# Softmax maximum taken as a minimum, and another order of two steps of the second layer

## The chip, the cores and the metric

The kernel runs on one core of a Trainium2 chip. The metric is the device time of one execution in microseconds (us); the median of three runs before the change is 1177.47 us. Engines are named as in the profile: PE (TensorE matmul), PEld (its weight loads), DVE (VectorE), ACT (ScalarE), POOL (GpSimd), SP (SyncE, which issues DMAs).

## The reference

Attention with a causal window of 128 and 4 sink positions (4 batches, 8 heads, 768 positions, head size 64), then two feed-forward layers on 3072 tokens of width 512: one dense, one with 8 experts of which each token takes one.

```python
scores = scale * q @ k.T                      # scale = 1/8
scores = where(is_sink | in_window, scores, -1e9)
a = exp(scores - max(scores)); a = a / (sum(a) + 1e-9)
x = (a @ v) as 3072 x 512
h = maximum(x @ w_in, 0); x = h * h @ w_out   # 512 -> 2048 -> 512
e = argmax(x @ w_gate)                        # 8 experts
y = maximum(x @ w1[e], 0) @ w2[e]             # 512 -> 1024 -> 512
out = softmax weight of e * sigmoid(x @ w_output_gate)[e] * y
```

## The kernel before

Matrices are float32. Products are made of three reduced-precision matmuls: each operand is split into a high part (a copy, mostly by ACT) and a remainder (a subtraction, mostly by DVE), and high x high, high x remainder and remainder x high are summed in PSUM.

**First layer.** The tokens go in 12 blocks `t` of 256; each block has attention for 4 head pairs `p` and two halves `n`, so 8 score steps, 96 in all. `scores` makes the products into PSUM (two heads `e`, up to 260 columns), adds the mask and takes the row maximum in one DVE instruction for each head (L425; the row value is written by a second, small DVE instruction under the same line), multiplies the two maxima by -SCALE (L427, DVE), takes the exponential with that as bias and sums the row (L429, ACT), adds 1e-9 (L431), inverts (L432), and scales the probabilities (L439 or L441). The sink columns go to `psk` (L444 to L446, POOL). `ptrans` transposes on PE (L458), `pv` multiplies by v (L499 or L492). `fin_sink` transposes `psk` (L516, PE) when the last of a block's 8 steps has filled it. The dense layer is `l1` (L566) and `l2` (L582), 16 steps a block, between which the attention of the next block is strewn by due times (`attn_events`, `run_to`). During block 0 the weights of the dense layer are converted, 32 pieces, each with three steps on ACT (L283, L284, L289; every third piece has the last one on DVE, L291), two on DVE (L286, L287) and one on POOL (L292). In this whole part the order on each engine is chosen by a planner from priorities and its own estimate of the times; `high_priority` blocks are moved ahead.

**Second layer.** The tokens are sorted by expert: `place` computes each token's place (PE L669 and L670, DVE L671 to L676) and POOL scatters the token numbers to the table `perm` (L678). `slots` computes which expert each of up to 31 slots of 128 tokens has. `places(s)` loads a slot's token numbers (SP, L855), `gather(s)` fetches the rows by an indirect DMA (POOL, L859), `xtr(s)` transposes them (PE L874, ACT L868, DVE L877), `m_l1` and `htr` make the hidden layer (PE L888, ACT L894; PE L901, ACT L868, DVE L904), `m_l2` the output (PE L917) whose second half scales it (ACT L925) and scatters the rows to the result (POOL L926). `split_raw` converts a quarter of the next expert's weights (DVE L841 and L842) and `load_raw` loads the following one (SP). This part stands under `manual_schedule`: each engine takes its instructions in the order of the code. Slots 0 and 1 are taken before all tokens are placed (they hold only tokens already placed); slot 2 (`PRE`) is the first that needs the last block's placing. The order around the change is L1048 to L1084.

A function given as `mid` to `m_l1` is called between the groups of three matmuls of one quarter of the inner dimension: before the change ahead of the third group.

Of the kernel before, what the change touches and what calls it, by code (L numbers as in the profile page):

```python
# [13 lines left out]
AF = mybir.ActivationFunctionType  # L14
ALU = mybir.AluOpType
# [12 lines left out]
SCALE = 1.0 / float(D) ** 0.5  # L28
# [14 lines left out]
def kern(ctx, tc, q, k, v, n_sink, window, w_in, w_out, w_gate, w_og, w1, w2, out):  # L43
    nc = tc.nc
    V, A, G, PE, SY = nc.vector, nc.scalar, nc.gpsimd, nc.tensor, nc.sync
# [36 lines left out]
    def fill(o, n):  # L82

        w = o.shape[-1]
        for _ in range(n):
            PE.matmul(o, lhsT=idle[:, 0:128], rhs=idle[:, 0:w], start=True, stop=True)
# [315 lines left out]
    def scores(t, p, n):  # L402
        i = 2 * (t % 3) + n
        W = 128 if i == 0 else 260
        c0 = KS * n if i else KS
        mask = (M0, M1, M2)[min(i, 2)]
        qt = qTt[t, p]
        kt = kTt[t, p]
        if t == 0 and n % 2:
            ps = [psX.tile([128, 512], F32, tag=f"x{e}", name=f"psx{e}") for e in range(2)]  # L410
        else:
            ps = [psS.tile([128, 260], F32, tag=f"s{e}", name=f"pss{e}") for e in range(2)]
        if t == 0:
            fill(ps[0][:, 0:W], 2)
        for e in range(2 if t < T32 else 0):
            r = slice(64 * e, 64 * e + 64)
            PE.matmul(ps[e][:, 0:W], lhsT=qt[r, 0, n, :].bitcast(F32), rhs=kt[r, 0, c0:c0 + W].bitcast(F32), start=True, stop=True)
        for m, (a_, b_) in enumerate(((0, 0), (0, 1), (1, 0)) if t >= T32 else ()):
            for e in range(2):
                r = slice(64 * e, 64 * e + 64)  # L420
                PE.matmul(ps[e][:, 0:W], lhsT=qt[r, a_, n, :], rhs=kt[r, b_, c0:c0 + W], start=(m == 0), stop=(m == 2))  # L421
        P = att.tile([128, 2, 260], F32, tag="P", name="P", bufs=2)
        st = att.tile([128, 8], F32, tag="st", name="st", bufs=4)
        for e in range(2):
            V.tensor_tensor_reduce(out=P[:, e, 0:W], in0=ps[e][:, 0:W], in1=mask[:, 0:W], scale=1.0, scalar=-3.0e38,  # L425
                                   op0=ALU.add, op1=ALU.max, accum_out=st[:, e:e + 1])
        V.tensor_scalar(out=st[:, 2:4], in0=st[:, 0:2], scalar1=-SCALE, scalar2=None, op0=ALU.mult)  # L427
        for e in range(2):
            A.activation(out=P[:, e, 0:W], in_=P[:, e, 0:W], func=AF.Exp, scale=SCALE, bias=st[:, 2 + e:3 + e],  # L429
                         accum_out=st[:, 4 + e:5 + e])  # L430
        V.tensor_scalar(out=st[:, 6:8], in0=st[:, 4:6], scalar1=1e-9, scalar2=None, op0=ALU.add)  # L431
        V.reciprocal(out=st[:, 6:8], in_=st[:, 6:8])  # L432
        if t >= T32 and i >= 2:

            V.tensor_tensor(out=P[:, :, 0:128], in0=P[:, :, 0:128], in1=P[:, :, 132:260], op=ALU.add)
            W = KS
        for e in range(2):
            if t < T32 and t + e:
                V.tensor_scalar(out=P[:, e, 0:W], in0=P[:, e, 0:W], scalar1=st[:, 6 + e:7 + e], scalar2=None, op0=ALU.mult)  # L439
            else:  # L440
                A.activation(out=P[:, e, 0:W], in_=P[:, e, 0:W], func=AF.Copy, scale=st[:, 6 + e:7 + e])  # L441
        if i >= 2:
            o = psk[n][:, 2 * p:2 * p + 2, :]
            G.tensor_copy(out=o[:, :, 0:4], in_=P[:, :, 128:132])  # L444
            G.tensor_copy(out=o[:, :, 8:12], in_=P[:, :, 128:132])
            G.tensor_tensor(out=o[:, :, 4:8], in0=P[:, :, 128:132], in1=o[:, :, 0:4].bitcast(F32), op=ALU.subtract)  # L446
        Ptile[t, p, n] = P
# [416 lines left out]
    def copy_out(o, i, branch):  # L864
        if branch:
            V.tensor_copy(out=o, in_=i)
        else:
            A.activation(out=o, in_=i, func=AF.Copy)  # L868

    def xtr(s, br=False):  # L870
        x = xg[s]
        ps = pC.tile([128, 4, 128], F32, tag="ht", name="psxt") if s < PRE else pA.tile([128, 4, 128], F32, tag="x", name="psxt")
        for kk in range(4):
            PE.transpose(ps[:, kk], x[:, 128 * kk:128 * kk + 128], ident[:])  # L874
        o = xtt[s % 2]
        copy_out(o[:, 0], ps[:], br)
        V.tensor_tensor(out=o[:, 1], in0=ps[:], in1=o[:, 0].bitcast(F32), op=ALU.subtract)  # L877
        xt2[s] = o

    def m_l1(s, n, par, br=False, mid=None):  # L880
        o = xt2[s]
        ps = pB.tile([128, 512], F32, tag="h", name="psh2")
        c = 0
        for kk in range(4):
            if kk == 2 and mid:
                mid()
            for a_, b_ in ((0, 0), (0, 1), (1, 0)):
                PE.matmul(ps[:], lhsT=o[:, a_, kk, :], rhs=wview(n, par + 2048 * b_ + 512 * kk, 512), start=(c == 0), stop=(c == 11))  # L888
                c += 1
        r = m3.tile([128, 512], F32, tag="r", name="r2", bufs=2)  # L890
        if br:
            V.tensor_scalar(out=r[:], in0=ps[:], scalar1=0.0, scalar2=None, op0=ALU.max)
        else:
            A.activation(out=r[:], in_=ps[:], func=AF.Relu)  # L894
        hh_[s, n] = r
# [149 lines left out]
    with tc.manual_schedule():  # L1045
        pt = lambda: pD.tile([128, 4, 128], F32, tag="y", name="psg2")
        tr, tr1, lg, place = gate_pieces(NBLK - 1, pt)
        xtr(0)  # L1048
        xtr(1)
        tr()  # L1050
        tr1()
        m_l1(0, 0, 0)
        m_l1(0, 1, 0, mid=lg)
        htr(0, 0)
        m_l1(1, 0, 0, mid=place)
        rest = slots(pt())
        extra = cv.tile([128, 2, XW], F32, tag="stage", name="xg2", bufs=3)
        xgr.extend(extra[:, n] for n in range(2))
        places(PRE)
        gather(PRE)  # L1060
        htr(0, 1)
        m_l1(1, 1, 0)
        rest()
        for s in range(PRE + 1, PRE + 6):
            places(s)
        m_l2(0, 0, 0)
        gather(3)
        htr(1, 0)
        split_raw(1, 4096)
        load_raw(1, es[2], True)  # L1070
        m_l2(0, 1, 0)
        htr(1, 1)
        gather(4)
        m_l2(1, 0, 0)
        xtr(2)
        split_raw(3, 4096)
        load_raw(3, es[2], True)
        m_l2(1, 1, 0)
        for n in range(2):
            m_l1(2, n, par_of(2))  # L1080
            resplit(2, n)
        xtr(3)
        htr(2, 0)
        htr(2, 1)  # L1084
        for s in range(2, NT // 128 - 1):
            body(s)
        s = NT // 128 - 1
        for n in range(2):
            m_l2(s, n, par_of(s))
            resplit(s, 2 + n)  # L1090
        tail(s + 1)
# [28 lines left out]
```

## Time and profile before

| | |
|---|---|
| median of three runs | 1177.47 us (1174.87 to 1177.99) |
| the profiled execution | 1176.28 us, span 1174.4 us |
| PE busy | 1127.7 us, 96% |
| DVE busy | 755.4 us, 64% |
| ACT busy | 633.6 us, 54% |
| POOL busy | 451.8 us, 38% |
| granted TensorE clock, mean | 0.987 |

PE is the engine with the largest share. The shares are means over stages: up to about 152 us block 0's attention, the conversion of the weights and block 0's products; then eleven blocks alike up to about 780 us; then the last block and the joint to the second layer, up to about 845 us; then one slot after another. A line of a stretch gives its length and for each engine the busy time and the number of instructions; PEclk is the granted clock as a share of full speed. In a timeline each row has its start, its duration, engine, line and operation, and in brackets the engine's idle time before it and what ended that.

### The profile page before, as it was taken

What the parts mean: (1) busy time and instruction counts of PE and PEld (TensorE: products, weight loads), DVE (VectorE), ACT (ScalarE), POOL (GpSimd) and SP (SyncE); (2) the same over time, 40 slices, a digit from 0 to 9 for tenths busy, and PEclk for the clock granted to TensorE, in tenths of its full rate; (3) what the DMA queues carried; (4) which work ended last, traced back from release to release, by engine and by line L of the source; (5) the groups of instructions that cost most, each with busy time, mean ns of one, the idle gap of its engine ahead of it and who ended that gap; (6) DMA issues with size and microseconds to landing.
All of it is one profiled execution on the core that took longest, in us unless ns stands there. A gap on an engine that the chain in (4) does not pass through costs nothing. (4 is left out here: it accounts for less than half of the span.)

```text
span 1174.4 us, 24093 instructions
## 1 busy us (share of the span) xinstructions
PE 1127.7 (96%) x7079; PEld 946.6 (81%) x7082; DVE 755.4 (64%) x2114; ACT 633.6 (54%) x1750; POOL 451.8 (38%) x949
## 2 busy tenths in 40 slices
PE   7888899999999999999999999999899999999996
PEld 3566688888888888888888888887688888888884
DVE  5899777667676767676667676557411566863153
ACT  4777676767676767676776667454222222222200
POOL 4466564336464326565335655210211221221111
PEclk9899999999999999999999999999999999999998
DMA  5666311111111111211111110295411366654110
GB/s 129 188 180 184 100 28 46 37 51 36 49 30 46 35 48 37 55 32 28 51 37 49 38 42 1 28 246 158 126 38 46 120 199 225 211 197 141 40 50 23
DMA packets 139388, 100.10 MB, mean 85 GB/s; under 512 B 103903, under 2 KB 112223, under 8 KB 139234
## 3 DMA queue, kind: packets, MB, share of 16 engines
q1 hardware_dynamic: 132674, 83.85, 25.9%
q0 software_dynamic: 5472, 14.19, 3.7%
q8 instruction: 65, 1.06, 0.4%
q14 instruction: 89, 0.73, 0.3%
q10 hardware_dynamic: 1088, 0.26, 0.1%
HBM read 85.56 MB, written 13.76 MB: 85 GB/s over the span
## 5 line engine op out<-in xcount | busy, mean ns | idle before, releaser
L566 PE MATMUL psh<-xT,WI 128*128 128x256 f32 x2304 | 314.3, 285 | 10.6 <-POOL WI L292 7.0
L566 PEld LDWEIGHTS psh<-xT,WI 128*128 128x128 f32 x2304 | 296.5, 191 | 26.4 <-POOL WI L292 9.1
L888 PE MATMUL psh<-WI,xt 128*128 (+1 forms) x672 | 164.8, 399 | 0.3 <-ACT ht L868 0.3
L582 PE MATMUL psx<-WOa,h 128*128 128x512 f32 x576 | 160.3, 411 | 0.0
L582 PE MATMUL psx<-WOb,h 128*128 128x512 f32 x576 | 157.1, 408 | 1.2 <-ACT h L572 0.9
L888 PEld LDWEIGHTS psh<-WI,xt 128*128 128x128 f32 x672 | 124.1, 188 | 28.1 <-ACT xt L868 0.5
L570 DVE TENSOR_TENSOR r<-r 128x256 f32<-128x256 f32 x184 | 88.0, 479 | 65.7 <-ACT r L569 65.4
L429 ACT ACTIVATE P<-P,st 128x260 f32<-128x260 f32 (+1 forms) x192 | 93.2, 486 | 50.4 <-DVE st L427 50.3
L582 PEld LDWEIGHTS psx<-WOb,h 128*128 128x128 f32 x576 | 102.2, 190 | 22.3 <-ACT h L572 2.4
L904 DVE TENSOR_TENSOR ht<-psht,ht 128x512 fp32r<-128x512 f32 x56 | 38.5, 689 | 124.4 <-ACT ht L868 124.0
L582 PEld LDWEIGHTS psx<-WOa,h 128*128 128x128 f32 x576 | 102.2, 191 | 19.1 <-issue 1.2
L573 DVE TENSOR_TENSOR h<-r,h 128x256 fp32r<-128x256 f32 x192 | 89.7, 467 | 32.3 <-ACT h L572 28.6
L569 ACT ACTIVATE r<-psh 128x256 f32<-128x256 f32 x192 | 71.9, 375 | 65.1 <-PE psh L566 62.5
L926 POOL DMA_INDIRECT out_dram<-xg,pidx x28 | 30.9, 1103 | 195.0 <-ACT xg L925 153.5
L474 POOL TENSOR_SCALAR_AFFINE_SELECT PT<-PT 128x256 fp32r<-128x256 f32 x224 | 86.6, 421 | 14.5 <-DVE st L427 12.7
L572 ACT ACTIVATE h<-r 128x256 fp32r<-128x256 f32 x192 | 78.1, 407 | 23.1 <-DVE r L570 17.8
L917 PE MATMUL psy<-WOb,ht 128*128 (+1 forms) x336 | 86.3, 406 | 0.0
L425 DVE CUSTOM_DVE_ANT_0 P<-pss,M 128x260 f32<-128x260 f32 (+1 forms) x184 | 72.7, 403 | 19.3 <-PE pss L421 7.3
L917 PE MATMUL psy<-WOa,ht 128*128 (+1 forms) x336 | 84.0, 397 | 0.0
L894 ACT ACTIVATE r<-psh 128x512 f32<-128x512 f32 x48 | 28.7, 598 | 99.9 <-PE psh L888 95.6
L859 POOL DMA_INDIRECT xg<-x2tab,pidx x30 | 36.7, 1225 | 100.0 <-issue 60.3
L917 PEld LDWEIGHTS psy<-WOa,ht 128*128 128x128 f32 x336 | 62.7, 188 | 14.7
(442 smaller groups left out, 1949.3 us busy)
## 6 DMA issues: line engine op xcount, KB each, us to landing
raw<-in_moe_w_dram SPq DMA_DIRECT2D x36, 1024.0 KB, 6.0
craw<-in_moe_w_in_dram SPq DMA_DIRECT2D x16, 512.0 KB, 4.1
craw<-in_moe_w_out_dram SPq DMA_DIRECT2D x16, 512.0 KB, 3.1
x2tab<-x2s SPq DMA_DIRECT2D x24, 256.5 KB, 3.6
kn<-in_k_dram SPq DMA_DIRECT2D x64, 96.0 KB, 2.2
vn<-in_v_dram SPq DMA_DIRECT2D x64, 96.0 KB, 2.2
qn<-in_q_dram SPq DMA_DIRECT2D x92, 64.0 KB, 2.1
kn<-in_k_dram SPq DMA_DIRECT2D x32, 64.0 KB, 2.0
```

Source lines behind the costliest of these rows:

```text
L425: V.tensor_tensor_reduce(out=P[:, e, 0:W], in0=ps[e][:, 0:W], in1=mask[:, 0:W], scale=1.0, scalar=-3.0e38, op0=ALU.add, op1=ALU.max, accum ...
L429: A.activation(out=P[:, e, 0:W], in_=P[:, e, 0:W], func=AF.Exp, scale=SCALE, bias=st[:, 2 + e:3 + e], accum_out=st[:, 4 + e:5 + e])
L474: G.affine_select(out=both[:, 1 - b, e], in_=bf[:, 0, e], pattern=[[0, 2], [1 - 2 * b, 128]], compare_op=ALU.is_gt if b else ALU.is_ge, fi ...
L566: PE.matmul(ps[:], lhsT=WI[:, j, a_, kk, :], rhs=x[:, b_, kk, :], start=(n == 0), stop=(n == 11))
L569: A.activation(out=hq[:], in_=ps[:], func=AF.Relu)
L570: (G if t == 0 and j % 2 else V).tensor_tensor(out=hq[:], in0=hq[:], in1=hq[:], op=ALU.mult)
L572: A.activation(out=o[:, 0], in_=hq[:], func=AF.Copy)
L573: V.tensor_tensor(out=o[:, 1], in0=hq[:], in1=o[:, 0].bitcast(F32), op=ALU.subtract)
L582: PE.matmul(acc[t][m][:], lhsT=o[:, a_, 128 * m:128 * m + 128], rhs=WO[j // 8][:, j % 8, b_, :], start=(j == 0 and n == 0), stop=(j == NF ...
L888: PE.matmul(ps[:], lhsT=o[:, a_, kk, :], rhs=wview(n, par + 2048 * b_ + 512 * kk, 512), start=(c == 0), stop=(c == 11))
L904: V.tensor_tensor(out=o[:, 1], in0=ps[:], in1=o[:, 0].bitcast(F32), op=ALU.subtract)
L917: PE.matmul(yp[s][:], lhsT=o[:, a_, kk, :], rhs=wview(2 + n, par + 2048 * b_ + 512 * kk, 512), start=(n == 0 and kk == 0 and c == 0), stop ...
```

## The change

Three edits. In `scores` the masked score is multiplied by -SCALE in the same instruction, and the row minimum is taken in place of the maximum; the step that multiplied the maxima is left out, and the exponential has the scale -1 and the minimum as bias. In `m_l1` the place at which `mid` is called becomes a parameter, and `place` is called ahead of the second group of slot 1 instead of the third. In the order of the second layer, `m_l2(1, 1, 0)` stands ahead of `xtr(2)`, `split_raw(3, 4096)` and `load_raw(3, ...)` instead of behind them.

```diff
         for e in range(2):
-            V.tensor_tensor_reduce(out=P[:, e, 0:W], in0=ps[e][:, 0:W], in1=mask[:, 0:W], scale=1.0, scalar=-3.0e38,
-                                   op0=ALU.add, op1=ALU.max, accum_out=st[:, e:e + 1])
-        V.tensor_scalar(out=st[:, 2:4], in0=st[:, 0:2], scalar1=-SCALE, scalar2=None, op0=ALU.mult)
+            V.tensor_tensor_reduce(out=P[:, e, 0:W], in0=ps[e][:, 0:W], in1=mask[:, 0:W], scale=-SCALE, scalar=3.0e38,
+                                   op0=ALU.add, op1=ALU.min, accum_out=st[:, e:e + 1])
         for e in range(2):
-            A.activation(out=P[:, e, 0:W], in_=P[:, e, 0:W], func=AF.Exp, scale=SCALE, bias=st[:, 2 + e:3 + e],
+            A.activation(out=P[:, e, 0:W], in_=P[:, e, 0:W], func=AF.Exp, scale=-1.0, bias=st[:, e:e + 1],
                          accum_out=st[:, 4 + e:5 + e])
...
-    def m_l1(s, n, par, br=False, mid=None):
+    def m_l1(s, n, par, br=False, mid=None, at=2):
...
-            if kk == 2 and mid:
+            if kk == at and mid:
                 mid()
...
-        m_l1(1, 0, 0, mid=place)
+        m_l1(1, 0, 0, mid=place, at=1)
...
         m_l2(1, 0, 0)
+        m_l2(1, 1, 0)
         xtr(2)
         split_raw(3, 4096)
         load_raw(3, es[2], True)
-        m_l2(1, 1, 0)
```

## Rows read from the trace of the kernel before

**Rows 1.** Busy time by stretch: start:end us, us, each engine's busy us, PEclk, DMA.

```profile
470.00:550.00 80.00, 79.56 (x577) 70.37 (x576) 56.28 (x198) 55.55 (x172) 46.46 (x122) 1.00 0.16 39
...
1000.00:1050.00 50.00, 50.00 (x241) 40.96 (x240) 35.48 (x29) 13.86 (x24) 11.66 (x7) 1.00 0.62 209
```

**Rows 2.** Busy time by stretch, the opening; columns as in the first group.

```profile
100.00:110.00 10.00, 7.93 (x49) 5.97 (x49) 10.00 (x22) 7.35 (x17) 6.85 (x8) 1.00 0.60 174
```

**Rows 3.** Waits of PE, 152 to 780 us: total us, times, longest.

```profile
PE psst L516 <- POOL psk L446: 2.6, 7, 0.5
```

**Rows 4.** PE in order of time: start us, us, what; in brackets idle before.

```profile
825.64 3.05 PE L917 MATMUL psy<-WOa,ht 128*128 128x512 f32 x12
832.21 1.11 PE L874 MATMUL psxt<-ident,xg 128*128 128x128 f32 x4 [3.53 <-DMA xg<-x2tab,pidx]
832.98 4.25 PE L917 MATMUL psy<-WOb,ht 128*128 128x512 f32 x12
837.07 5.76 PE L888 MATMUL psh<-WI,xt 128*128 x24
842.67 0.60 PE L874 MATMUL psxt<-ident,xg 128*128 128x128 f32 x4
```

**Rows 5.** Line 427 alone by stretch: us, DVE busy us (count), PEclk, DMA.

```profile
0.00:53.00 53.00, 1.62 (x10) 0.94 0.62 166
53.00:152.00 99.00, 4.01 (x9) 0.93 0.50 144
```

**Rows 6.** Line 425 over the span: duration of one, ns, min/median/max.

```profile
L425 DVE CUSTOM_DVE_ANT_0 P<-pss,M x184: 278/429/431, 15.5 to 734.4; 128x260 f32<-128x260 f32 x152, 128x128 f32<-128x128 f32 x32
```

**Rows 7.** DVE in order of time, a steady softmax.

```profile
306.83 0.08 DVE L425 DVE_READ_ACCUMULATOR2_ANT st<- 128x1 f32 x1
...
307.17 0.16 DVE L427 TENSOR_SCALAR st<-st 128x2 f32<-128x2 f32 x1
307.23 0.42 DVE L372 TENSOR_TENSOR qT<-psq,qT 128x256 fp32r<-128x256 f32 x1
```

**Rows 8.** ACT in order of time, the same softmax.

```profile
306.80 0.39 ACT L371 ACTIVATE qT<-psq 128x256 fp32r<-128x256 f32 x1 [0.81 <-PE psq L360]
307.36 0.52 ACT L429 ACTIVATE P<-P,st 128x260 f32<-128x260 f32 x1 [0.18 <-DVE st L427]
```

**Rows 9.** DVE in order of time, the opening.

```profile
108.97 1.27 DVE L427 TENSOR_SCALAR st<-st 128x2 f32<-128x2 f32 x1
110.16 0.15 DVE L431 TENSOR_SCALAR st<-st 128x2 f32<-128x2 f32 x1
```

**Rows 10.** POOL in order of time, the same stretch.

```profile
108.49 1.72 POOL L292 TENSOR_TENSOR WOb<-fbuf,WOb 128x512 fp32r<-128x512 f32 x1 [1.62 <-ACT WOb L289]
```

**Rows 11.** DVE in order of time, at the second layer's placing.

```profile
814.36 0.69 DVE L904 TENSOR_TENSOR ht<-psht,ht 128x512 fp32r<-128x512 f32 x1 [0.33 <-ACT ht L868]
814.97 0.15 DVE L671 TENSOR_TENSOR cum<-cum,oh 128x8 bf16<-128x8 bf16 x1
```

**Rows 12.** DVE in order of time, remainders of slots 1 and 2.

```profile
827.78 0.68 DVE L904 TENSOR_TENSOR ht<-psht,ht 128x512 fp32r<-128x512 f32 x1
833.99 0.69 DVE L877 TENSOR_TENSOR xt<-psxt,xt 128x512 fp32r<-128x512 f32 x1 [5.53 <-ACT xt L868]
```

**Rows 13.** ACT in order of time, the copy of slot 2's transposes.

```profile
833.36 0.60 ACT L868 ACTIVATE xt<-psxt 128x512 fp32r<-128x512 f32 x1 [6.70 <-PE psxt L874]
```

**Rows 14.** Busy time by stretch after three waits of PE; PEclk follows POOL.

```profile
88.10:91.50 3.40, 3.40 (x14) 3.01 (x13) 3.40 (x10) 2.88 (x5) 1.41 (x1) 0.50 0.50 153
106.90:110.30 3.40, 3.38 (x20) 2.97 (x20) 3.40 (x10) 2.25 (x5) 1.72 (x1) 1.00 0.48 116
832.20:835.60 3.40, 3.39 (x10) 2.90 (x11) 1.61 (x2) 0.60 (x1) 0.00 (x0) 0.50 0.83 256
```

**Rows 15.** PE in order of time, two waits of the opening.

```profile
87.63 2.13 PE L566 MATMUL psh<-xT,WI 128*128 128x256 f32 x10 [0.93 <-POOL WI L292]
...
106.92 1.44 PE L566 MATMUL psh<-xT,WI 128*128 128x256 f32 x10 [1.08 <-POOL WI L292]
```

## The prediction

> **What bounds the kernel now.** I read the busy times by stretch first. In the steady first layer PE is busy 79.56 of 80 us and in the second layer 50.00 of 50, both at the full granted clock, while DVE has a third of its time left over [rows 1]. So in these stretches only what makes PE wait, or gives PE more to do, counts. That leaves three places. The opening, up to some 152 us, where attention of the first blocks, the conversion of the weights and the first multiplications share DVE: there DVE is busy all 10 us of a stretch in which PE reaches 7.93 [rows 2]. The few waits of PE inside the steady stage, read from PE's list of waits [rows 3]. And the joint between the layers, read from PE in order of time: one wait of 3.53 us for the gather of slot 2's tokens, with slow matmuls behind it [rows 4].
>
> **Part 1, softmax.** The change removes line 427 once for each of 96 score steps, 19 of them before 152 us [rows 5], 77 after. The exponential no longer waits for that step, and its first half only for the first half's minimum. Nothing is added: line 425 keeps its count and form, the scale is now a constant other than 1, and the exponential still reads one pointer (the bias). That a minimum takes as long as a maximum no row shows; I take the 429 ns of the maximum [rows 6], because only the comparison differs, and keep a dearer minimum as a rival.
>
> In the steady stage the step is hidden: PE is full. The exception is the sink transposes, for which PE waits 2.6 us in 7 waits [rows 3], on POOL, which waits for the last softmax of its block. There the second accumulator is read out by 306.83 + 0.08 = 306.91, line 427 starts at 307.17 and the next DVE step at 307.23 [rows 7]; ACT starts the exponential at 307.36, but had other work until 306.80 + 0.39 = 307.19 [rows 8]. So the exponential can come 307.36 - 307.19, some 0.2 us earlier, a little more because consecutive ACT steps overlap; I take 0.23. Seven times that is 1.6 us. Ends: 0 if another step is late next (DVE's sum or POOL's three small steps), 2.6 if all seven waits go.
>
> In the opening I count places in DVE's queue. The next step starts 0.06 us after line 427's start [rows 7], so 19 places are 1.1 us. The upper end is their whole busy time, 1.62 + 4.01 = 5.6 us [rows 5]. The gap between the two is mostly a few long ones: at 108.97 one took 1.27 us. But it ended at 110.24, with the POOL step that ran from 108.49 to 110.21 [rows 9, 10]; without line 427 the next DVE step, line 431 or a two-input step of the weight conversion, would stand there and end no sooner. So I take 1.1 us. The order of the opening is a planner's, and removing a step lets it choose another order in the neighbourhood; the lower end is therefore below nothing, by the slow stretches of the rivals.
>
> The Trainium skill has rules on both. "SBUF — State Buffer", section Who interferes with whom, says that a tensor_scalar and a POOL instruction exclude each other for the whole instruction, and that a two-input DVE instruction meets POOL's reads in the same way: by that the stall passes to the next step, which speaks against this change, and the 1.27 us row ends with POOL's as the rule has it. "VectorE: DVE Perf Modes", section The DRAIN you can't avoid, has the next operation wait until the pipe is empty, so that each removed one would give back its whole duration, 19 x 0.16 = 3.0 us; the rows show the next one starting after 0.06.
>
> **Part 2, the placing three matmuls earlier.** PE computes the places one group of three matmuls sooner, about 0.7 us (24 matmuls take 5.76, [rows 4]). I cost this at nothing, because DVE takes the places up in order: the remainder of slot 0's first half holds DVE from 814.36 to 815.05 and the first placing step starts at 814.97, as that ends [rows 11]. If that cover were gone, the index, the scatter, the list and the gather of slot 2 would come up to 0.7 us earlier; that is the upper end.
>
> **Part 3, slot 1's second product ahead of slot 2's transposes.** Before: slot 1's first product ends at 825.64 + 3.05 = 828.69, PE waits until 832.21, transposes, multiplies from 832.98, and starts slot 2 at 837.07 [rows 4]. After: the second product follows the first at once. Its input's remainder is ready at 827.78 + 0.68 = 828.46 [rows 12], so it can, with 0.2 us to spare. It takes 3.05 as its twin at full clock, less the 0.2 by which consecutive matmul groups overlap, and ends about 831.5. The gather lands at 832.21 as before: POOL's queue up to it is unchanged. The transposes take 0.60 at full clock [rows 4], until 832.81. ACT starts the copy 0.04 after the transposes' end (832.21 + 1.11 = 833.32 against 833.36) and takes 0.60 [rows 13]: 833.45, and PE about 833.5. The third matmul needs DVE's remainder, which started 0.63 after the copy's start and took 0.69 [rows 12, 13]: 832.85 + 0.63 + 0.69 = 834.17, while two matmuls of 0.24 bring PE to 833.98: 0.2 lost. Slot 2 effectively starts at 833.7 instead of 837.07: 3.4 us gained.
>
> This adds a wait: PE stands about 0.7 us for the gather and 0.7 for the copy, with all of slot 2 and everything behind it queued. What moves with the product: on ACT the scaling of slot 1's output, now ahead of slot 2's copy; it would run from about 831.6 to 832.3, before the copy is due. On POOL the scatter of slot 1, which is moved past no POOL step: the gather of slot 4 stands before it in both orders. On DVE and SP nothing passes anything: slot 2's remainder, then the conversion of a weight quarter, then its reload, some tenths of a us earlier. Behind this joint PE is full [rows 1], so the gain is carried to the end.
>
> What bounds it: of the 3.4 us, (4.25 - 3.05) + (1.11 - 0.60) = 1.7 is the slow matmuls behind the wait [rows 4]; the granted clock of 832.20 to 835.60 was 0.50, the 1.2 GHz level, and PE had been idle for 3.53 before [rows 14]. The new waits are shorter, but short waits too were followed by half clock once: after one of 0.93 us ten matmuls took 2.13 us, granted 0.50, whereas after one of 1.08 ten took 1.44 at full clock [rows 14, 15]. If it falls anyway, 1.7 us go and 1.7 remain; if the placing does help, up to 4.1. I take 3.4, because the two waits are nearer to the 0.9 to 1.1 us kind than to the long one and that kind fell in one of two.
>
> **Sum.** 3.4 + 1.6 + 1.1 = 6.1 us. The profiled execution took 1176.28 us (span 1174.4), 1.2 below the median of the runs: it would become 1170.2, and the median 1177.47 would become 1171.4.
>
> **The rivals.**
> Only the joint pays. The planner's new order gives the opening's places back and another step is late at the sinks: 3.4 us, 1174.1; with a half clock behind the joint as well, 1175.8. For it: at the sinks several steps follow the exponential; in the opening the stalls pass on. Against: PE's seven waits are on this chain.
> The opening pays whole. Exponentials come earlier, the attention of the first blocks with them, and DVE's 5.6 us [rows 5] all leave the path where DVE is full [rows 2]: 6.1 + 4.5 = 10.6, 1166.9. Against it stands the row that ends with POOL's.
> The opening is ordered worse. PE finds two more half-clock stretches of about 1.7 us each: 3.4 + 1.6 - 3.4 = 1.6, 1175.9. For it: the opening already has such a stretch after short waits [rows 14].
> Slower: the minimum is dearer. If the minimum took twice the time, the 38 instructions of the opening would add 38 x 0.43 = 16 us to an engine that is full there [rows 2, 6]; on the path whole, that is 1177.5 - 6.1 + 16.3 = 1187.7. It makes the kernel slower from 0.16 us more for each (6.1 / 38). Against it: one comparison in place of another.
>
> **How the numbers follow.** Chances: forecast 0.50 (1171.4); only the joint 0.24; the opening whole 0.10; the opening worse 0.12; the minimum dearer 0.04. A measurement of this kernel can tell some 0.3%, 3.5 us, from no change: the border lies at 1173.9. Of the forecast 0.47 lies below it, of the opening whole 0.10, of only the joint 0.06: faster 0.63. Same: the rest of these, and the opening worse: 0.32. Slower 0.05. The range 1166.5 to 1176.2 takes in the whole opening, both ends of the joint and the sinks and the worse order, and leaves the dearer minimum and some tails out.
>
> **What would show it.** Line 425 at 429 ns with no line 427; PE's waits on the sink transposes at about 1.0 us instead of 2.6; slot 1's second product starting at once after the first; waits of some 0.7 us for the gather and then for the copy, full granted clock, and 3.4 us less up to slot 2's first matmul; the first placing step still on the heels of slot 0's remainder. I am wrong if the stretch up to 152 us moves by more than 3 us either way, if the clock falls at the joint, or if line 425 is longer.

## The result, and the profile after

The changed kernel takes 1168.24 us (median, 1165.58 to 1171.37) beside 1177.22 us for the kernel before on the same chip: ratio 0.9912 over all runs, interval 0.9898 to 0.9927 (the two medians alone give 0.9924). That is faster by just under 1%, clear of the noise, and 3.2 us below the forecast of 1171.4. The profiled execution has a span of 1166.5 us where the one before had 1174.4, so 7.9 us have to be found.

Lines are numbered one lower in the changed kernel from the exponential on (it is L428, the scaling of the probabilities L440, the sink's POOL steps L443 to L445, the sink transposes L515).

Cut at four milestones of PE, the two profiled executions compare as follows. The opening ends with block 2's first dense-layer matmul, the steady part with the start of the dense layer's last weight load, the joint with that of slot 2's first weight load.

| us | opening | steady | joint | rest |
|---|---|---|---|---|
| before | 206.45 | 597.47 | 32.92 | 337.59 |
| after | 206.92 | 592.10 | 29.79 | 337.70 |
| difference | +0.5 | -5.4 | -3.1 | +0.1 |
| forecast | -1.1 | -1.6 | -3.4 | 0 |

In the old order PE loads slot 2's first weights 0.23 us ahead of its first matmul, in the new one both start together. Counted on to the start of slot 3's transposes, where that no longer matters, the gain behind the dense layer is 38.74 - 35.75 = 3.0 us.

**The joint.** PE of after in order of time (start us, busy us, what; in brackets the idle time before, and what ended it):

```profile
820.72 3.05 PE L916 MATMUL psy<-WOa,ht 128*128 128x512 f32 x12
823.61 2.96 PE L916 MATMUL psy<-WOb,ht 128*128 128x512 f32 x12
827.47 0.66 PE L873 MATMUL psxt<-ident,xg 128*128 128x128 f32 x4 [0.90 <-DMA xg<-x2tab,pidx]
828.82 6.12 PE L887 MATMUL psh<-WI,xt 128*128 x24 [0.69 <-ACT xt L867]
834.77 0.60 PE L873 MATMUL psxt<-ident,xg 128*128 128x128 f32 x4
```

The second product follows the first at once, the wait of 3.53 us [rows 4] has become one of 0.90 for the gather and one of 0.69 for ACT's copy, and no matmul is slow. The window right behind shows the clock (us, then busy time of PE, weight loads, DVE, ACT and POOL, then the granted clock, DMA share, GB/s):

```profile
827.40:830.80 3.40, 2.64 (x11) 1.76 (x12) 1.97 (x3) 0.60 (x1) 0.03 (x1) 1.00 0.83 239
```

1.00 is the 2.4 GHz level; the window behind the long wait of before had 0.50 [rows 14]. The 24 matmuls of slot 2 take 6.12 instead of 5.76 us [rows 4], 0.36 more: 0.15 of it ahead of the third, which waits for DVE's remainder of the transposed tokens, and 0.10 each ahead of the second and the fourth, for which the profile names no wait. From slot 2's transposes to slot 3's it was 842.67 - 832.21 = 10.46 us before [rows 4] and is 834.77 - 827.47 = 7.30 now.

**The placing.** DVE of after in order of time: the first placing step (L670) starts at 810.06, just as the remainder of slot 0's first half ends (810.14), as in [rows 11]. The earlier matmuls are hidden there.

```profile
809.45 0.69 DVE L903 TENSOR_TENSOR ht<-psht,ht 128x512 fp32r<-128x512 f32 x1 [0.33 <-ACT ht L867]
810.06 0.15 DVE L670 TENSOR_TENSOR cum<-cum,oh 128x8 bf16<-128x8 bf16 x1
```

**The minimum.** One line's summary (duration of one in ns, min/median/max): as long as the maximum, 429 before [rows 6].

```profile
L425 DVE CUSTOM_DVE_ANT_0 P<-pss,M x184: 277/428/432, 15.1 to 730.6; 128x260 f32<-128x260 f32 x152, 128x128 f32<-128x128 f32 x32
```

**The steady part.** PE's whole list of waits between 152 and 780 us in after (total us, times, longest) has no line for the sink transposes any more:

```profile
PE pso L498 <- POOL PT L473: 0.4, 1, 0.4
PE psc L696 <- DVE x2U L621: 0.4, 1, 0.4
PE psk__3149 L329 <- DVE PT L477: 0.2, 1, 0.2
PE psk__8901 L329 <- DVE PT L477: 0.2, 1, 0.2
PE psk__6025 L329 <- DVE PT L477: 0.2, 1, 0.2
```

In [rows 3] that line had 2.6 us. But the steady part gave 5.4, and the order of PE's instructions in it is the same in both kernels, so every microsecond can be booked by the time from the start of one matmul to the start of the next. Booked to the later of the two, the steady part's 12 sink transposes fell from 5.37 to 2.06 us, the 160 transposes of keys and queries (L329 and L360; called key transposes below, since every wait among them is at L329) from 24.76 to 23.35, and everything else from 567.3 to 566.7: 3.3 + 1.4 + 0.7 = 5.4. Only the first two stand clear of the scatter: in executions with the same order on every engine they agree within 0.1 us, but everything else differs by up to 1.2 (567.3 to 568.5 in four with the old softmax). All 14 sink transposes from 152 us on (two of them lie in the opening), counted from the start of each, fell from 5.11 to 0.95 us: 4.16, where the list shows 2.6. The list counts a wait only from the modelled end of the matmul before, and hides the part of it that lies under that end; the rows of before below show it, 0.71 us from start to start and 0.44 in brackets.

One steady softmax, the place of [rows 7, 8]. After, DVE, ACT, POOL and PE in order of time:

```profile
305.84 0.51 ACT L428 ACTIVATE P<-P,st 128x260 f32<-128x260 f32 x1
...
306.43 0.43 DVE L425 CUSTOM_DVE_ANT_0 P<-pss,M 128x260 f32<-128x260 f32 x1
...
306.91 0.51 ACT L428 ACTIVATE P<-P,st 128x260 f32<-128x260 f32 x1 [0.47 <-DVE st L425]
...
307.42 0.36 ACT L371 ACTIVATE qT<-psq 128x256 fp32r<-128x256 f32 x1
...
309.26 0.44 POOL L445 TENSOR_TENSOR psk<-P,psk 128x8 fp32r<-128x8 f32 x1
...
310.16 0.38 PE L515 MATMUL psst<-ident,psk 128*128 128x128 f32 x2
```

The end of it before, PE and POOL:

```profile
310.20 0.27 PE L516 MATMUL psst<-ident,psk 128*128 128x128 f32 x1
...
310.37 0.49 POOL L446 TENSOR_TENSOR psk<-P,psk 128x8 fp32r<-128x8 f32 x1
...
310.91 0.33 PE L516 MATMUL psst<-ident,psk 128*128 128x128 f32 x1 [0.44 <-POOL psk L446]
```

The first head's exponential starts at 305.84, before the second head's minimum (306.43) has begun; before, it stood behind both maxima and the scaling step, at 307.36 [rows 8]. The sink's three POOL steps are done by 309.26 + 0.44 = 309.70, and PE is not there until 310.16: 0.46 us of slack. Before, PE was there at 310.20 and waited between its two transposes until POOL was done at 310.86.

### The profile page after: what moved, and what is told of

Read it like the earlier page. It is cut to its first block, busy times and chain, and to the rows that moved or that the text cites. A ratio compares the mean times of both kernels' runs of the same rounds, so it can differ in the third digit from the quotient of the medians.

```text
span 1166.5 us, 23899 instructions
## 1 busy us (share of the span) xinstructions
PE 1127.8 (97%) x7082; PEld 947.2 (81%) x7082; DVE 739.7 (63%) x2018; ACT 637.1 (55%) x1750; POOL 468.5 (40%) x949
## 5 line engine op out<-in xcount | busy, mean ns | idle before, releaser
L569 DVE TENSOR_TENSOR r<-r 128x256 f32<-128x256 f32 x184 | 86.3, 470 | 118.1 <-ACT r L568 117.3
L903 DVE TENSOR_TENSOR ht<-psht,ht 128x512 fp32r<-128x512 f32 x56 | 38.5, 689 | 123.6 <-ACT ht L867 123.2
L428 ACT ACTIVATE P<-P,st 128x260 f32<-128x260 f32 (+1 forms) x192 | 93.8, 489 | 34.9 <-DVE st L425 34.1
L572 DVE TENSOR_TENSOR h<-r,h 128x256 fp32r<-128x256 f32 x192 | 93.5, 487 | 19.0 <-ACT h L571 13.6
L473 POOL TENSOR_SCALAR_AFFINE_SELECT PT<-PT 128x256 fp32r<-128x256 f32 x224 | 98.1, 471 | 15.1 <-DVE PT L469 14.8
L440 ACT ACTIVATE P<-P,st 128x132 f32<-128x132 f32 (+2 forms) x168 | 62.2, 415 | 35.3 <-DVE st L431 34.1
L508 POOL TENSOR_TENSOR xr<-tB,tC 128x128 f32<-128x128 f32 x80 | 37.7, 471 | 101.3 <-DVE tB L507 96.6
```

The costliest lines, as they stand in the source:

```text
L473: G.affine_select(out=both[:, 1 - b, e], in_=bf[:, 0, e], pattern=[[0, 2], [1 - 2 * b, 128]], compare_op=ALU.is_gt if b else ALU.is_ge, fi ...
L569: (G if t == 0 and j % 2 else V).tensor_tensor(out=hq[:], in0=hq[:], in1=hq[:], op=ALU.mult)
L572: V.tensor_tensor(out=o[:, 1], in0=hq[:], in1=o[:, 0].bitcast(F32), op=ALU.subtract)
```

## The experiments

Ratios are to the kernel before, run beside each on the same chip. All stage times below are cut as in the table above.

### The change in its parts

The softmax edit alone:

```diff
-  scale=1.0, scalar=-3.0e38, op0=ALU.add, op1=ALU.max, ...
-V.tensor_scalar(out=st[:, 2:4], in0=st[:, 0:2], scalar1=-SCALE, ...)
+  scale=-SCALE, scalar=3.0e38, op0=ALU.add, op1=ALU.min, ...
-A.activation(..., func=AF.Exp, scale=SCALE, bias=st[:, 2 + e:3 + e], ...)
+A.activation(..., func=AF.Exp, scale=-1.0, bias=st[:, e:e + 1], ...)
```

> The kernel before with the softmax edit alone. Theory: the steady stage (block 2's first matmul to the last of the dense layer, 597.5 us before, 592.1 after) falls by the same 5.4 us, because PE no longer waits at the sink transposes and at three of the six key transposes; the joint (last of the dense layer to slot 2's first matmul, 32.9 us before) stays. Time 5 to 6 us below before. Rival (my forecast's size): 1.6 us in the steady stage, the rest of the 5.4 belonging to something else, time 2.7 us below before. In both the opening may move by a few us either way.

1170.65 us, ratio 0.9935 (0.9913 to 0.9957), 7.7 us where 5 to 6 were expected, which the interval takes in. Steady 592.19, sinks 0.95 (here and below all 14, from the start of each): the steady gain is this edit's, whole. The joint (33.07) stays as before.

Both edits of the second layer alone:

```diff
-m_l1(1, 0, 0, mid=place)
+m_l1(1, 0, 0, mid=place, at=1)
...
 m_l2(1, 0, 0)
+m_l2(1, 1, 0)
 xtr(2)
...
-m_l2(1, 1, 0)
```

> The kernel before with both edits of the second layer and the old softmax. Theory: all stages up to the joint as before to within 0.3 us, the joint 3.0 to 3.4 us shorter, nothing given back later: 3.0 to 3.4 us below before. Rival: the clock falls at the two short waits and only 1.7 us remain. Rival: the order change is given back at a later gather or weight reload, time as before.

1176.09 us, ratio 0.997 (0.9952 to 0.9988). Joint 30.03: the joint's gain is this edit's. Steady 598.31, 0.8 more than in the kernel before with the same order on every engine: so much differs from one execution to the next. Of 1177 us, the two ratios are 7.7 and 3.5 us, together 11.2, and the whole change 10.4: the parts add up within their intervals.

The other order alone:

```diff
 m_l2(1, 0, 0)
+m_l2(1, 1, 0)
 xtr(2)
...
-m_l2(1, 1, 0)
```

> The kernel before with slot 1's second product moved ahead of slot 2's transposes, and nothing else. Theory: the placing edit does nothing, since DVE takes the places up only after the remainder of slot 0's first half; so this equals the run with both edits of the second layer to within 0.2 us in the joint, 3.0 to 3.4 us below before. Rival: the placing edit brings the gather earlier by up to 0.7 us, and this run's joint is 0.5 to 0.7 us longer than with both.

1174.93 us, ratio 0.9971 (0.9953 to 0.9989), the same as with the placing edit. Its joint is 30.28 us, 0.25 longer and so a little outside the expected 0.2; its index was ready no later, the gather landed later.

And the placing edit alone:

```diff
-m_l1(1, 0, 0, mid=place)
+m_l1(1, 0, 0, mid=place, at=1)
```

> The kernel before with the places computed one group of matmuls earlier, and nothing else. Theory: no change (0 within 0.2 us in the joint); the gather of slot 2 lands at the same distance from the first layer's end, PE still waits 3.5 us. Rival: the gather lands 0.5 to 0.7 us earlier and the time falls by as much.

1178.3 us, ratio 0.999 (0.9974 to 1.0006): nothing that can be measured. The index is ready 11.88 to 11.90 us behind the last dense-layer weight load with and without it. The joint of the profiled execution is 33.99 us, longer than before's and not within the expected 0.2; half clock lasted 6.8 us there, twice as long as before.

The swap alone met half clock all the same. Its PE from slot 2's transposes on, and the window behind it (columns as above):

```profile
836.05 0.66 PE L874 MATMUL psxt<-ident,xg 128*128 128x128 f32 x4 [1.40 <-DMA xg<-x2tab,pidx]
837.40 7.67 PE L888 MATMUL psh<-WI,xt 128*128 x24 [0.69 <-ACT xt L868]
```

```profile
838.10:841.50 3.40, 3.40 (x9) 2.70 (x9) 3.37 (x2) 0.00 (x0) 0.00 (x0) 0.52 0.84 308
```

The granted clock is 0.52, near the 1.2 GHz level, after waits of 1.40 and 0.69 us; 24 matmuls take 7.67 us where after has 6.12. So the new order can meet it too. Over all profiled executions, half clock fell within slot 1's second product and slot 2's start in six of eight with the old order and in one of six with the new one.

That allows the joint's gain to be cut in two. From slot 2's transposes to slot 3's, the old order at full clock took 8.90 us (the first and the third kernel of the next section), with half clock 10.46 [rows 4]; the new order 7.30 at full clock. So the order itself is worth 1.60 us and the clock 1.56 (2.5 and 2.7 in the two executions where half clock lasted 6.8 us).

### What in the softmax edit pays

A scaling step for each head in place of the common one, directly behind its maximum:

```diff
 for e in range(2):
     V.tensor_tensor_reduce(..., op1=ALU.max, accum_out=st[:, e:e + 1])
+    V.tensor_scalar(out=st[:, 2 + e:3 + e], in0=st[:, e:e + 1], scalar1=-SCALE, ...)
-V.tensor_scalar(out=st[:, 2:4], in0=st[:, 0:2], scalar1=-SCALE, ...)
```

> The kernel before, with the scaling step done for each head by itself right behind its own maximum: one DVE instruction more in each score step, and the first exponential waits for the first maximum alone. Theory (what helps is that the first exponential no longer waits for the second maximum): PE's waits at the sink transposes, 2.6 us in 7 in the list before, go as they went in the changed kernel, and the steady stage is 3 to 5.4 us shorter than 597.5 us although DVE has 96 instructions more. Rival (what helps is the removed step and its place in DVE's queue): the waits stay or grow, the steady stage is 597.5 us or longer.

1181.63 us, ratio 1.0049 (1.0029 to 1.0069): slower. The sinks did fall, from 5.11 to 3.47, but the key transposes' waits rose from 2.38 (6 of them) to 6.08 (11), and the steady part to 600.79. Why, the last two experiments of this section show.

The new softmax with the scaling step still there, its result read by nobody:

```diff
   scale=-SCALE, scalar=3.0e38, op0=ALU.add, op1=ALU.min, ...
+V.tensor_scalar(out=st[:, 2:4], in0=st[:, 0:2], scalar1=-SCALE, ...)
```

> The kernel with the softmax edit alone, and the old scaling step put back in its place, but nobody reads its result. Theory (waits): steady stage 592 to 593 us as with the softmax edit alone. Rival (DVE's queue): the steady stage goes back towards 597.5 us, by half of the 5.4 or more. The opening, where DVE is full, may lose 1 to 2 us by 19 steps.

1170.67 us, ratio 0.9955 (0.9942 to 0.9968); steady 592.17, sinks 0.95. The instruction costs nothing in the steady part; what paid is that nobody waits for it.

The two heads' exponentials written in the other order:

```diff
-for e in range(2):
+for e in (1, 0):
     A.activation(..., func=AF.Exp, scale=-1.0, bias=st[:, e:e + 1], ...)
```

> The kernel with the softmax edit alone, but the second head's exponential is taken first, so that both exponentials come after both minima; no instruction is added or removed. Theory: the chain is longer by one exponential of 0.5 us than with the softmax edit alone, the waits at the sink transposes come back in part, 0.1 to 0.3 us each, and the steady stage is 0.7 to 2 us longer than 592.1. Rival (the removed step alone makes the gain): as with the softmax edit alone to within 0.3 us.

1168.32 us, ratio 0.994 (0.9917 to 0.9963); steady 592.22. The expected loss did not come, but the experiment did not do what it says: the planner chooses the order on each engine, and on ACT the first exponential again starts ahead of the second minimum (at 303.77, the minimum at 304.36). PE, DVE, POOL and SyncE have the order of the softmax edit alone, ACT differs in one place in the opening. It is that kernel a second time, and leaves the question open.

So the next one ties both exponentials to the second minimum by data:

```diff
-A.activation(..., func=AF.Exp, scale=-1.0, bias=st[:, e:e + 1], ...)
+A.activation(..., func=AF.Exp, scale=-1.0, bias=st[:, 1:2], ...)
```

> The new softmax alone (layer 2 as in the kernel before), but both heads' exponentials take the second head's minimum as their bias, so that neither can start before it; the shifts then differ from the heads' own maxima, which leaves the quotients as they are. No scaling step. In the profiles the sink's chain (second minimum to sink transposes) is 1.1 us shorter after than before; 0.4 of it is the scaling step (0.48 us from the second minimum's start to the exponential behind it, 0.88 before), 0.5 the first head's exponential, which no longer stands behind the second minimum. POOL is then done 0.46 us ahead of the first sink transpose. Theory (the change is worth what PE waited, the rest of the chain's gain is slack): the 0.5 us given back here is nearly covered by the slack, the 14 sink transposes stay under 1.8 us from start to start (5.1 before, 0.95 after), the steady blocks take 592.2 to 593.5 us (597.5 to 598.7 before, 592.1 to 592.2 with the whole edit), ratio 0.993 to 0.996. Rival (most of the gain comes from the first head's exponential being let go, and the scaling step is worth only the forecast's 0.23 us a place): sinks 3 us or more, steady blocks 595 to 597 us, ratio 0.9965 to 0.9985. Rival (any change of the schedule would have freed the sinks): as the theory, with no order between the sinks' waits and the chain's length.

1183.13 us, ratio 1.0029 (1.0013 to 1.0046): slower than before, which no theory had expected. The sinks took 3.13 us, about half way between 5.11 and 0.95, as the first rival had it: 2.0 us of the sinks' gain is the scaling step, 2.2 the first exponential. My own account of the slack was off in one number: from the second minimum's start to POOL's end it was 308.84 to 312.85 = 4.01 us, 0.74 longer than in after (3.27) and not 0.5, because the reciprocal also came later. 0.74 less 0.46 of slack leaves 0.28, and the pair of transposes stood 0.71 us where after has 0.38.

The total, however, went the other way: steady 602.31. PE's order is that of before, one matmul apart, and the excess is at the key transposes: 30.22 us booked to them instead of 24.76. At 534.63 PE waited for a DVE step. The POOL step and the square on DVE 3.5 us earlier, and PE, in order of time:

```profile
530.89 1.17 POOL L623 TENSOR_TENSOR x2U<-x2U,x2T 128x512 bf16<-128x512 f32 x1 [1.43 <-ACT x2T L622]
...
531.11 1.22 DVE L569 TENSOR_TENSOR r<-r 128x256 f32<-128x256 f32 x1 [0.97 <-ACT r L568]
...
534.63 0.55 PE L329 MATMUL psk__8175<-ident,kn 128*128 128x128 f32 x3 [0.71 <-DVE PT L469]
```

The square (L569, both operands in SBUF) takes 1.22 us; its median is 0.425. It ends 0.27 us behind POOL's end, and everything behind it in DVE's queue is 0.8 us late. This is the mechanism that the forecast read at one place of the opening [rows 9, 10]. In this kernel 11 of the 14 key waits come 3.5 to 3.6 us behind such a square, in the one with a scaling step for each head all 11 (3.7 us behind), and in the kernel before all 6 (3.6). Not every such square costs PE something: the first two of these kernels have 17 over 1.0 us each in the steady part, and six of the 17 have no key wait behind them. The kernel before:

```profile
587.42 1.16 POOL L624 TENSOR_TENSOR x2U<-x2U,x2T 128x512 bf16<-128x512 f32 x1 [5.09 <-ACT x2T L623]
...
587.65 1.22 DVE L570 TENSOR_TENSOR r<-r 128x256 f32<-128x256 f32 x1 [0.97 <-ACT r L569]
...
591.22 0.44 PE L329 MATMUL psk__9196<-ident,kn 128*128 128x128 f32 x2 [0.25 <-DVE PT L478]
```

In after one square of 160 is longer than 1.0 us and 14 take 0.60 to 0.83, and no key wait follows any of them; with the unread scaling step none is over 1.0. To see whether this is the cause, the next kernel cuts only that POOL step (in all blocks but the last, where DVE does it):

```diff
 (the kernel above)
-G.tensor_tensor(out=c, in0=r, in1=b, op=ALU.subtract)
+for i in range(4):
+    w = slice(128 * i, 128 * i + 128)
+    G.tensor_tensor(out=c[:, w], in0=r[:, w], in1=b[:, w], op=ALU.subtract)
```

> The kernel with both exponentials behind the second minimum, and one edit more: POOL's step that takes the gate's second remainder (128x512) is cut into four of 128 columns; the order on PE, DVE and ACT stays the same, row for row. That kernel's steady blocks took 602.3 us against 597.5 before, and 5.5 us of that stands ahead of the key transposes. In the traces 11 of its 14 key-transpose waits come 3.5 us behind a square step of DVE that took 1.22 us instead of 0.43, each beside this POOL step (1.17 us, begun 0.23 us earlier); in the kernel before all 6 key waits do, in the kernel with a scaling step for each head all 11. Theory (DVE's step with two operands in SBUF stands until POOL's step ends): with quarters of some 0.3 to 0.5 us the square takes under 0.85 us, the 11 waits shrink by 0.4 us or more each (key waits 7.2 us to under 3.5 us), the 14 sink transposes stay near 3.1 us, and the steady blocks take 597 to 599 us; ratio to before 0.998 to 1.000. Rival (DVE is late there for the order of its own steps, and POOL's length has no part in it): squares may shorten, but key waits stay at 6 to 7 us and the steady blocks at 601 to 603 us, ratio 1.002 to 1.004.

1175.64 us, ratio 0.9973 (0.9961 to 0.9986). Steady 596.69 instead of 602.31, with the same order on PE, DVE and ACT. The place of the rows above in this kernel:

```profile
526.65 1.96 POOL L625 TENSOR_TENSOR x2U<-x2U,x2T 128x128 bf16<-128x128 f32 x4 [1.43 <-ACT x2T L622]
...
526.88 0.48 DVE L569 TENSOR_TENSOR r<-r 128x256 f32<-128x256 f32 x1 [0.97 <-ACT r L568]
...
529.69 0.55 PE L329 MATMUL psk__8214<-ident,kn 128*128 128x128 f32 x3
```

POOL starts 0.23 us ahead of the square as before, but the square takes 0.48, and the key transposes have no wait. No square is over 1.0 us any more, the 11 waits are gone and the three others stay (1.82 us), and the sinks stay at 3.00. The theory holds, and the steady part came 0.3 us below its range. What the steady part's time is made of in the four kernels (us from matmul start to matmul start, booked to the later):

| | sink transposes | key transposes | all else | key waits |
|---|---|---|---|---|
| before | 5.37 | 24.76 | 567.3 | 2.38 (6) |
| both behind the second minimum | 3.69 | 30.22 | 568.4 | 7.18 (14) |
| the same, POOL's step in quarters | 3.55 | 24.77 | 568.4 | 1.82 (3) |
| after | 2.06 | 23.35 | 566.7 | 1.17 (3) |

From before to the quartered kernel the steady part falls by 597.47 - 596.69 = 0.8 us, and from there to after by another 4.6. These are not the prices of the scaling step and of the first exponential: the quartered kernel has POOL's step changed as well, and "all else" scatters by 1.2 us. What can be told apart is in the first two columns.

### Can the joint give more

In after PE still waits 0.90 us for the gather of slot 2. The placing step put ahead of slot 0's first-half transposes:

```diff
-htr(0, 0)
 m_l1(1, 0, 0, mid=place, at=1)
+htr(0, 0)
```

> The changed kernel, with the transposes of slot 0's first hidden half moved behind slot 1's first product with its placing, so that DVE's placing steps no longer stand behind that half's remainder. Theory: the places are ready 0.9 to 1.0 us earlier, the gather of slot 2 lands as much earlier, PE's wait of 0.9 us for it goes, and slot 2 starts 0.8 to 0.9 us earlier: 0.8 us below the changed kernel. Rival: the scatter of the places or the list's load sets the gather's time and it lands no earlier: 0. Rival: the first output product now waits for slot 0's late first half and loses what the gather gains.

1167.33 us, ratio 0.9922 (0.9898 to 0.9946): the time of after. The index was ready 1.0 us earlier and the list 1.3, but the joint took 30.19 us. PE, DVE and POOL of this kernel in order of time:

```profile
811.63 0.69 DVE L903 TENSOR_TENSOR ht<-psht,ht 128x512 fp32r<-128x512 f32 x1 [2.49 <-ACT ht L867]
...
821.42 2.29 DVE L841 TENSOR_TENSOR WI<-raw,WI 128x2048 fp32r<-128x2048 f32 x1
...
821.76 2.81 POOL L858 DMA_INDIRECT xg<-x2tab,pidx  x1 [10.12 <-DMA pidx<-perm]
...
822.82 0.63 PE L916 MATMUL psy<-WOb,ht 128*128 128x512 f32 x2
...
823.63 0.68 DVE L903 TENSOR_TENSOR ht<-psht,ht 128x512 fp32r<-128x512 f32 x1
...
824.37 2.59 PE L916 MATMUL psy<-WOb,ht 128*128 128x512 f32 x10 [0.92 <-DVE ht L903]
```

The gather's POOL step, issued during DVE's weight conversion (L841), took 2.81 us; the next, without that neighbour, 0.97. The gather landed 28.80 us behind the last dense-layer weight load instead of 28.40. And DVE, which now stood 2.49 us for slot 0's late first half, ran 1.5 us later from there on: the conversion, ahead of the remainder (L903) in both kernels, began 23.16 us behind that weight load instead of 21.66, and slot 1's second product waits 0.92 us for the remainder. The gain was eaten on DVE.

So the next kernel keeps this edit and gives the conversion's rounding copy to ACT, where there is room:

```diff
 m_l1(1, 1, 0)
+A.activation(out=wview(1, 4096, 2048), in_=src1, func=AF.Copy)
 rest()
...
-split_raw(1, 4096)
+V.tensor_tensor(out=wview(1, 6144, 2048), in0=src1, in1=<the copy>, op=ALU.subtract)
```

> The kernel after, with the placing step ahead of slot 0's first-half transposes as in the kernel with that edit alone, and with the rounding copy of the weight quarter that DVE converts in slot 1 moved to ACT, behind slot 1's second ReLU, where ACT is idle for 2.4 us (such a copy takes ACT 1.9 us in the profile of before); DVE keeps the remainder. Theory (in the kernel with the placing edit alone, the list came 1.3 us earlier, but DVE's two conversion steps of 1.20 and 2.29 us held up the last remainder, for which PE waited 0.92 us, and stood beside the gather's POOL step, which took 2.81 us instead of 0.98): without the 1.20 us step the remainder is 1.2 us earlier, PE has no wait in slot 1's last product, POOL's step ends 1.2 us earlier, slot 2's first matmul is 28.6 to 29.2 us behind the last dense-layer weight load (29.8 after, 30.2 with the placing edit alone, when no half clock falls there), and the time is 0.6 to 1.3 us below that of the kernel after. Rival (the gather's transfer, not DVE, ends last): start of slot 2 unchanged at 29.8 to 30.2, same time as after within 0.3 us. Rival (ACT's copy holds up slot 1's work on ACT or reads beside DVE's small steps): slower than after.

The kernel after, beside it:

> The kernel after unchanged, beside the other two on the same chip: 0.991 to 0.993 of before by every theory, joint of 29.7 to 31.3 us by whether the clock falls there.

1168.59 us, ratio 0.9905 (0.9876 to 0.9935), and 1167.85, ratio 0.9903 (0.9876 to 0.993) for the kernel after, just under the expected 0.991 to 0.993. In the profiles the joint is 29.00 us against 29.82, as the theory had it, and slot 1's second product has no wait:

```profile
824.38 2.96 PE L916 MATMUL psy<-WOb,ht 128*128 128x512 f32 x12
827.49 0.66 PE L873 MATMUL psxt<-ident,xg 128*128 128x128 f32 x4 [0.15 <-DMA xg<-x2tab,pidx]
```

But the expected 0.6 to 1.3 us in the time cannot be told: each ratio is known only to 0.3%, 3.5 us. The openings of these two executions were 206.94 and 205.50 us and differ by more than the joints do. It is not shown to beat the kernel after.

## Why the forecast was right, and where not

**What bounds the kernel.** Right: PE's order did not change in the steady part, and the gains that stand clear of the scatter are waits of PE's that went and, at the joint, slow matmuls behind one.

**The joint, 3.4 forecast, 3.1 measured.** Right in mechanism and in both halves: 1.7 us for the slow matmuls (1.56 measured) and 1.7 for the order (1.60). The two short waits were put at 0.7 us each and are 0.90 and 0.69; ACT's copy and DVE's remainder are where they were expected; 0.36 us were lost at slot 2's first matmuls instead of 0.2, and the gather landed 0.16 us later, counted from the last dense-layer weight load, not as before. That makes the 3.0 us to slot 3's transposes. That the clock stays full behind short waits held in five of six executions with the new order, so it is likely, not certain.

**The placing, 0.** Right, and for the reason given: the first placing step starts on the heels of slot 0's remainder. With that remainder moved away, in the kernel with the placing first, the index was ready 1.0 us earlier.

**The minimum.** Right: 428 ns against 429.

**The opening, 1.1.** Not shown. Old softmax: 206.45, 206.50, 208.43 and 206.88 us, mean 207.1; the new one with the second layer either way, the kernel after and its relatives whose softmax is the same: 206.92, 205.06, 204.85, 206.15, 206.94 and 205.50, mean 205.9. The difference of 1.2 would fit, but like kernels scatter by up to 2 us, with 17 to 24 us of half clock in each opening. Against the forecast's reason, places in DVE's queue, stands the kernel with the unread scaling step: it has all of these places back, and its opening was the shortest, 204.49 us, though in one execution. The rival with the whole 5.6 us is not seen.

**The sinks, 1.6 forecast, 5.4 us measured for the steady part.** This is the term that was mis-sized, in three ways.

First, the price of one place. The text said that the first half's exponential would wait only for the first half's minimum, and then priced only the scaling step, 0.23 us. That step by itself was priced about right: with the exponentials tied, the sinks lost 5.11 - 3.13 = 2.0 us, 0.28 for each of seven places. But the first exponential, 0.52 us of ACT's time [rows 8], left the chain altogether, and that was worth as much again: the sinks' 4.16 us are 0.59 for each place. Nor did the bound of 0.2 us hold, which ACT's other step (L371) set [rows 8]: in after it stands behind both exponentials, at 307.42.

Second, the upper end. 2.6 us was taken as all that the seven waits hold [rows 3]; measured from matmul start to matmul start they held over 4.

Third, waits that were not on that list's first line. The key transposes waited six times, 2.38 us, because a square step on DVE stood 1.22 us beside a POOL step. After has no such wait; three others, 1.17 us, came. This gain is the order's, not the edit's by design: tied exponentials came with 11 of them, 5.6 us of steady time, by the same planner. The forecast allowed the planner such freedom in the opening alone. That the collision causes the waits is shown by the quartered POOL step; for the kernel before and the one with a scaling step for each head it rests on the same rows, 6 of 6 and 11 of 11.

The Trainium skill has the rule: "SBUF — State Buffer", section Who interferes with whom, says that a DVE instruction with two SBUF inputs and a POOL instruction that reads SBUF stand in each other's way: whichever is issued first keeps the other waiting for the whole instruction. The traces agree: POOL 0.23 us ahead, the square 1.22 instead of 0.43 us, done 0.27 us behind POOL's step. The forecast used this rule to say that a stall passes on to the next step, which it read at one place of the opening; it did not look for it in the steady part.

**The time.** That 1168.24 fell in the range of 1166.5 to 1176.2 is in part luck. The range's lower end came from an opening that pays whole, which is not seen; with the forecast's own upper ends for the other terms, 4.1 at the joint, 2.6 at the sinks and 1.1 in the opening, it would have ended at 1177.47 - 7.8 = 1169.7, above the time measured. The sinks' miss was covered by room meant for something else.

**What stays open.** How much of the 4.6 us between the quartered kernel and after is the chain, how much the planner's other order on DVE and ACT, and how much scatter (the "all else" column moves by 1.7 us), was not separated; at the sinks alone the first exponential is worth about 2. The quartered POOL step was not tried on the kernel after, where only one square is over 1.0 us.

## What to carry to other kernels

Where two halves of a chain share one small step, ask first which half it holds back from starting at all: letting one half run ahead was worth as much at the sinks as the step itself. Measure a wait of PE from matmul start to matmul start, in kernels with the same order, before taking the list of waits as the most that can be won. And where a planner orders the engines, look in the new trace for steps of two or three times their median length beside a step of another engine: such collisions came and went with edits that have nothing to do with them, and cost more than the edits.

## What the runs showed of the hardware

A gather's step on POOL took 2.81 us where DVE had begun a step of 2.29 us with two SBUF operands 0.34 us ahead of it, and ended 0.86 us behind that step; the next took 0.97. It is no single case: in the kernel after, six gather steps between 941 and 1029 us were issued while such a DVE step ran, took 1.99 to 3.03 us, and ended 0.85 to 1.52 us behind it; where the DVE step began with the gather's or after it, in 88 places over all profiles behind 800 us, the gather took 0.97 to 1.11. Cutting a POOL step of 1.17 us into four of 0.43 to 0.61 made it longer as a whole (1.96 us) and the DVE step beside it shorter by 0.74. And half clock behind a wait did not follow the wait's length alone: with the old order two of eight executions kept full clock, behind waits of 2.85 and 3.25 us, while another had half clock at one of 3.24; with the new one of six lost it behind 1.40 and 0.69.
